# The first microseconds of an attention and feed-forward kernel: other queues, another order, other dummy matmuls

## The chip, the cores and the metric

The kernel runs on one core of a Trainium2 chip (trn2). The metric is the time of one execution in device microseconds (us); lower is better. The core's engines work side by side, each through its own list of instructions in order: TensorE (PE in the profile, with PEld for its weight loads), VectorE (DVE), ScalarE (ACT), GpSimd (POOL) and SyncE (SP). DMA transfers are issued by POOL, SP and ACT from those same lists; an issue that waits holds up everything behind it on its engine.

## The reference

Two stages follow each other. The first is a linear attention over 8 batches, 8 heads, 576 positions and 64 numbers per head; the second is a feed-forward layer with a squared ReLU.

```python
def phi(x):                                   # x: q or k
    proj = np.einsum('bhsd,df->bhsf', x, w_phi)           # 64 -> 128
    proj = proj - np.max(np.abs(proj), axis=-1, keepdims=True)
    return np.concatenate([np.exp(proj), np.exp(-proj)], axis=-1)
q_p, k_p = phi(q), phi(k)
kv = np.einsum('bhsf,bhsd->bhfd', k_p, v)
z = np.sum(k_p, axis=2)
num = np.einsum('bhsf,bhfd->bhsd', q_p, kv)
den = np.einsum('bhsf,bhf->bhs', q_p, z)[..., None] + 1e-06
x = (num / den)            # -> 4608 tokens x 512
h = np.maximum(x @ w_in, 0.0)                 # w_in: 512 x 2048
out = (h * h) @ w_out                         # w_out: 2048 x 512
```

All inputs and the output are float32; the kernel computes in bfloat16 with float32 sums.

## The kernel before, in words

**Stages.** `attention(b)` handles one batch: it transposes k and q so that the 64 numbers of a head lie on partitions, projects them with `w_phi` (the bfloat16 copy `wphi2` holds it twice, in partitions 0 to 63 and 64 to 127, so that two heads can be projected side by side), takes maxima on VectorE (`Mk`, `Mq`), exponentials on ScalarE (`Ekp`, `Ekn`), multiplies with v (`V`, `KV`), and forms the attention's output `xo`, which is transposed into `xT`. The feed-forward layer works on chunks of 512 tokens: `F1`/`f1` groups (matmuls of `win` and `xT`), ReLU and square, `F2` groups (`h` and `wout`). The attention of batch b+1 is interleaved with the feed-forward layer of the chunks before it.

**Transposes.** For batches 0 and 1, k and q are transposed on TensorE with an identity matrix `ident` (L320). From batch 2 on, SP issues transposing DMAs: kT<-xk and qT<-xq (L331). The output of batch 0 is transposed on TensorE, that of later batches by transposing DMAs xT<-xo (L708). `xo` has three buffers.

**Loads.** q, k, v, `w_in` and `w_out` are loaded by POOL, which casts them to bfloat16 on the way; at most eight of its loads are under way, each new one waits for the one eight places earlier. `xk`, `xq` and `xv` have two buffers each, so the load of batch 2 follows the last use of batch 0. Only the first heads of batch 0's k take another way: two float32 halves (128 KB each) come into the idle output buffer `ot[2]` by plain DMAs, and one `kcast` for each half turns them into bfloat16, the first on VectorE, the second on ScalarE. `w_phi` comes by a plain DMA from SP; two `wcast` write its two bfloat16 copies.

**Order.** Every operation has a number, in the order in which the program adds it. `ORDER` is a list of these numbers, written out, and `pin` chains the instructions of each engine in that order; `STATES` chooses between VectorE and ScalarE for some operations, `BASES` gives the PSUM banks, `GATES` gives some loads an operation to wait for. `FILL` puts a number of dummy matmuls (L961, on a zeroed tile `warm`) on TensorE ahead of an operation.

**The start.** In the order before: SP issues w_phi; ACT issues both k halves; POOL issues k (heads 4 to 7), q (first half), k (heads 2 and 3), then makes `ident` (L913) from a tile that VectorE zeroed (L238), then issues the second half of q, and so on. VectorE zeroes `warm`, casts the first k half, zeroes `ident`, does both `wcast`. TensorE runs 26 dummy matmuls, the four transposes of the first heads, 11 more dummies, and projects (L379).

The numbers that the diff moves: 0 and 1 are the k halves (`xkh`), 2 is w_phi, 3 and 4 the two `wcast`, 5 the zeroing of `ident`, 6 that of `warm`, 7 and 8 the two `kcast`, 11 `ident`, 12 to 14 POOL's first loads (13 is k of heads 4 to 7, 14 q, 12 k of heads 2 and 3). 303 and 304 are the two parts of the first-layer group on w_in's columns 0 to 511 for the first 128 tokens, 307/308 and 311/312 those on the next columns (512 to 1023, 1024 to 1535); 139 is a transpose of `xo`, 162, 148, 164 and 150 are L648 groups (`NA`, `NB`), 163 and 149 the scalings on VectorE (`SA`) between an `NA` and its `NB`.

Of the kernel before, what the change touches and what calls it, by code (L numbers as in the profile page):

```python
# [24 lines left out]
def dve_cost(n):  # L25
    return n / 960 + 0.064, n / 960 + 0.150 + SEM
# [82 lines left out]
def kernel(  # L109
# [10 lines left out]
    nc = tc.nc  # L120
# [97 lines left out]
    for hi in range(2):  # L218
        def fn(hi=hi):
            pin(nc.scalar.dma_start(out=ot[2][:, 256 * hi : 256 * hi + 256],  # L220
                            in_=k[0][hi, 0:512, :].rearrange("(p j) d -> p (j d)", j=4)))
        add("ACT", (0.4, 2.85), fn, w=[("xkf", hi)], what="xkh")
# [5 lines left out]
    for half in (1, 0):  # L228
        def f_wcast(half=half):
            pin(nc.vector.tensor_copy(out=wphi2[half * 64 : half * 64 + 64, :], in_=wphi_f[0:64, :]))  # L230
        add("DVE", dve_cost(64), f_wcast, r=["wphi_f"] + [("wphi2", 1)] * (1 - half), w=[("wphi2", 1) if half else "wphi2"],
            what="wcast")
# [875 lines left out]
```

## Time and profile before

| | |
|---|---|
| time, median of 3 runs | 344.13 us |
| the runs | 344.02 to 344.96 us |
| profiled execution, span from first to last instruction | 344.8 us |
| its own time beside the span | not listed apart; the span lies within the runs |
| PE busy | 335.5 us (97%) |
| DVE, ACT, POOL busy | 264.2, 225.4, 95.5 us |
| mean granted TensorE clock | 0.998 |
| HBM read, written | 36.73 MB, 9.44 MB |

In lists by time, the first number is the start in us from the start of the span, the second the time from the first start to the last end, then engine, line, operation, output<-input and the number of instructions; square brackets hold the idle time before and what ended it. "SPq" and "POOL ... DMA_DIRECT2D" are times of issuing; the transfer lands later. In lists of waits, the numbers are the total, the count and the longest wait. In lists of DMA issues the last number is the time from the start of the issue to landing, in us. Rows by stretch end with the granted clock, the share of the DMA engines and GB/s.

### The profile page before, as it was taken

What the parts mean: (1) busy time and instruction counts of PE and PEld (TensorE: products, weight loads), DVE (VectorE), ACT (ScalarE), POOL (GpSimd) and SP (SyncE); (2) the same over time, 40 slices, a digit from 0 to 9 for tenths busy, and PEclk for the clock granted to TensorE, in tenths of its full rate; (3) what the DMA queues carried; (4) which work ended last, traced back from release to release, by engine and by line L of the source; (5) the groups of instructions that cost most, each with busy time, mean ns of one, the idle gap of its engine ahead of it and who ended that gap; (6) DMA issues with size and microseconds to landing.
All of it is one profiled execution on the core that took longest, in us unless ns stands there. A gap on an engine that the chain in (4) does not pass through costs nothing.

```text
span 344.8 us, 8417 instructions
## 1 busy us (share of the span) xinstructions
PE 335.5 (97%) x3389; PEld 188.3 (55%) x3389; DVE 264.2 (77%) x485; ACT 225.4 (65%) x393; POOL 95.5 (28%) x143
## 2 busy tenths in 40 slices
PE   8999999799999999999999999999999999999995
PEld 7679776444654555545545554565555444444443
DVE  4999999699877987788898999687876635757510
ACT  4999996489898898476887797798475503210031
POOL 8670671681730390104604051240000000000000
PEclk9999999999999999999999999999999999999999
DMA  9999999999999999999999999999864821101024
GB/s 139 179 206 202 199 132 157 153 118 205 170 175 172 227 165 185 195 182 183 171 207 172 199 164 195 188 154 168 196 125 96 157 62 38 63 0 61 32 68 115
DMA packets 142935, 51.51 MB, mean 149 GB/s; under 512 B 111472, under 2 KB 138416, under 8 KB 142896
## 3 DMA queue, kind: packets, MB, share of 16 engines
q1 hardware_dynamic: 97488, 32.35, 50.7%
q0 software_dynamic: 44960, 18.23, 46.7%
q8 instruction: 26, 0.43, 0.5%
q10 hardware_dynamic: 448, 0.39, 0.4%
q14 instruction: 13, 0.11, 0.1%
HBM read 36.73 MB, written 9.44 MB: 134 GB/s over the span
## 4 chain that ended last, share of the span: by engine, by line
PE 87%; DMA 6%; DVE 3%; ACT 1%; POOL 1%; issue 0%; POOLq 0%; DVEq 0%; SPq 0%
PE psum L788 32%; PE psum L882 31%; PE psum L648 5%; PE psum L462 5%; PE psum L347 5%; DMA xT<-xo 4%; DMA qpn<-qf 3%; PE psum L827 2%; PE psum L569 1%; DVE mk L405 1%; PE psum L813 1%; PE psum L799 1%; PE psum L846 1%; PE psum L450 1%; PE psum L320 1%; PE psum L961 1%
## 5 line engine op out<-in xcount | busy, mean ns | idle before, releaser
L882 PE MATMUL psum<-wout,h 128*128 128x512 bf16 x560 | 132.6, 380 | 0.0
L788 PE MATMUL psum<-xT,win 128*128 128x512 bf16 x448 | 106.1, 379 | 0.6 <-DMA xT<-xo 0.6
L765 ACT ACTIVATE hr<-psum 128x512 bf16<-128x512 f32 x98 | 57.1, 600 | 57.7 <-PE psum L788 50.2
L882 PEld LDWEIGHTS <-h 128*128 128x128 bf16 x560 | 51.1, 98 | 56.5 <-issue 0.3
L788 PEld LDWEIGHTS <-win 128*128 128x128 bf16 x512 | 46.7, 97 | 51.9 <-DMA xT<-xo 1.4
L774 DVE TENSOR_TENSOR h<-hr 128x512 bf16<-128x512 bf16 x144 | 56.0, 415 | 18.7 <-ACT hr L765 18.2
L544 ACT ACTIVATE qf<-psum 128x1024 bf16<-128x1024 f32 (+1 forms) x50 | 46.1, 939 | 5.5 <-PE psum L347 2.0
L405 DVE TENSOR_REDUCE mk<-psum 128x8 f32<-128x1024 f32 (+1 forms) x38 | 42.4, 1120 | 3.9 <-PE psum L347 2.0
L411 ACT ACTIVATE kn<-psum 128x1024 bf16<-128x1024 f32 (+1 forms) x38 | 35.7, 948 | 8.2 <-PE psum L347 4.7
L411 ACT ACTIVATE kp<-psum 128x1024 bf16<-128x1024 f32 (+1 forms) x38 | 35.8, 951 | 4.8 <-PE psum L347 4.0
L648 PEld LDWEIGHTS <-qpn 128*128 128x128 bf16 x624 | 27.5, 97 | 16.6 <-issue 3.1
L767 DVE TENSOR_SCALAR hr<-psum 128x512 bf16<-128x512 f32 x46 | 31.1, 684 | 5.7 <-PE psum L788 4.2
L660 DVE TENSOR_TENSOR psum<-psum,en 128x520 f32<-128x520 f32 (+1 forms) x39 | 27.2, 702 | 10.3 <-PE psum L648 6.1
L648 PE MATMUL psum<-kv,qpn 128*128 128x65 bf16 x624 | 30.6, 193 | 2.5 <-DVE xo L674 2.4
L269 POOL DMA_DIRECT2D xq<-in_q_dram x24 | 17.3, 727 | 55.2 <-DVE h L774 14.3
L531 DVE TENSOR_REDUCE mq<-psum 128x8 f32<-128x1024 f32 (+1 forms) x25 | 27.8, 1112 | 3.3 <-PE psum L347 2.5
L674 DVE TENSOR_TENSOR xo<-psum,rden 128x512 bf16<-128x512 f32 (+1 forms) x39 | 26.4, 684 | 3.7 <-DMA xT<-xo 3.2
L249 POOL DMA_DIRECT2D xk<-in_k_dram x27 | 20.0, 744 | 32.5 <-ACT en L508 16.0
L584 ACT ACTIVATE qpn<-psum 128x1024 bf16<-128x1024 f32 (+1 forms) x30 | 26.8, 955 | 2.5 <-PE psum L569 2.2
L195 ACT ACTIVATE ot<-psum 128x512 f32<-128x512 f32 x24 | 14.4, 598 | 20.3 <-PE psum L882 20.1
L428 DVE TENSOR_TENSOR va<-xv,va 128x1280 bf16<-128x1280 bf16 (+2 forms) x34 | 23.4, 714 | 0.8 <-ACT va L420 0.8
L249 POOL DMA_DIRECT2D xv<-in_v_dram x27 | 19.9, 744 | 14.7 <-PE psum L788 11.1
(79 smaller groups left out, 348.9 us busy)
## 6 DMA issues: line engine op xcount, KB each, us to landing
out_dram<-ot SPq DMA_DIRECT2D x32, 256.0 KB, 2.9
xk<-in_k_dram POOLq DMA_DIRECT2D x25, 128.0 KB, 5.6
xq<-in_q_dram POOLq DMA_DIRECT2D x24, 128.0 KB, 4.5
xv<-in_v_dram POOLq DMA_DIRECT2D x24, 128.0 KB, 5.0
win<-in_moe_w_in_dram POOLq DMA_DIRECT2D x4, 512.0 KB, 9.8
wout<-in_moe_w_out_dram POOLq DMA_DIRECT2D x4, 512.0 KB, 15.1
xq<-in_q_dram POOLq DMA_DIRECT2D x4, 256.0 KB, 6.4
out_dram<-ot SPq DMA_DIRECT2D x6, 128.0 KB, 2.3
```

What stands on the lines that cost most here:

```text
L249: pin(nc.gpsimd.dma_start(out=x[:, m0 + a * 512 : m0 + z * 512].rearrange("p (h x) -> p h x", x=4 * D), in_=src[b][2 * a : 2 * z, 0:512, : ...
L405: pin(nc.vector.tensor_reduce(out=mk_view(g), in_=ps2(pj)[:, :, : n * Fd].rearrange("p e (i f) -> p e i f", f=Fd), axis=AX.X, op=ALU.max, ...
L411: pin(nc.scalar.activation(out=dst[slot][:, :, :n, :].rearrange("p e i f -> p e (i f)"), in_=ps2(pj)[:, :, : n * Fd], func=ACT.Exp, scale= ...
L531: pin(nc.vector.tensor_reduce(out=mqb[:, c, :, :n], in_=ps2(pj)[:, :, : n * Fd].rearrange("p e (i f) -> p e i f", f=Fd), axis=AX.X, op=ALU ...
L544: pin(nc.scalar.activation(out=o, in_=i_, func=ACT.Exp, scale=sgn))
L648: pin(nc.tensor.matmul(out=o[:, u // 4, u % 4 * D1 : (u % 4 + 1) * D1], lhsT=qpn[slot][:, sg * half + u * m : sg * half + u * m + P], rhs= ...
L660: pin(nc.vector.tensor_tensor(out=o, in0=o, in1=enb[:m, c, :].rearrange("t (b h) -> t b h", b=2).to_broadcast([m, 2, 4, D1]), op=ALU.mult))
L765: pin(nc.scalar.activation(out=hr[sl], in_=ps1(g), func=ACT.Relu))
L767: pin(nc.vector.tensor_scalar(out=hr[sl], in0=ps1(g), scalar1=0.0, scalar2=None, op0=ALU.max))
L774: pin(nc.vector.tensor_tensor(out=dst, in0=i_, in1=i_, op=ALU.mult))
L788: pin(nc.tensor.matmul(out=o, lhsT=win[mc // 4][:, kc, mc % 4 * P : (mc % 4 + 1) * P], rhs=x, start=(kc == 0), stop=(kc == KC - 1)))
L882: pin(nc.tensor.matmul(out=ps1(g), lhsT=h2[c % 2][mc // 4][:, mc % 4, tt * P : (tt + 1) * P], rhs=wout[mc // 4][:, mc % 4, :], start=(mc = ...
```

## The change

The second k half is issued by SP and w_phi behind it; VectorE zeroes `ident` before its cast; POOL makes `ident` behind its first load instead of its third; the first of the two `wcast` (the one for partitions 64 to 127) runs on ScalarE behind the `kcast` there; seven of the numbers of dummy matmuls differ, 17 fewer in all; and on TensorE the first-layer group 303/304 runs before 311/312 instead of after `NA` 162. Nothing else in `ORDER` differs.

```diff
     for hi in range(2):
         def fn(hi=hi):
-            pin(nc.scalar.dma_start(out=ot[2][:, 256 * hi : 256 * hi + 256],
+            pin((nc.scalar, nc.sync)[hi].dma_start(out=ot[2][:, 256 * hi : 256 * hi + 256],
                             in_=k[0][hi, 0:512, :].rearrange("(p j) d -> p (j d)", j=4)))
-        add("ACT", (0.4, 2.85), fn, w=[("xkf", hi)], what="xkh")
+        add(("ACT", "SP")[hi], (0.4, 2.85), fn, w=[("xkf", hi)], what="xkh")
...
     for half in (1, 0):
         def f_wcast(half=half):
-            pin(nc.vector.tensor_copy(out=wphi2[half * 64 : half * 64 + 64, :], in_=wphi_f[0:64, :]))
-        add("DVE", dve_cost(64), f_wcast, ...
+            copy(wphi2[half * 64 : half * 64 + 64, :], wphi_f[0:64, :])
+        add("ACT" if half else "DVE", act_cost(128) if half else dve_cost(64), f_wcast, ...
...
 ORDER = [
-    2, 0, 1, 13, 14, 12, 8, 6, 7, 5, 3, 4, 11, 19, 40, 41, ...
+    1, 0, 2, 6, 5, 13, 11, 14, 12, 8, 7, 3, 4, 19, 40, 41, ...
...
-    307, 308, 221, 147, 139, 311, 312, 309, 144, 233, 162, 313, 303, 140, 163, 304, 223, 148, 141, 164, ...
+    307, 308, 221, 147, 139, 303, 304, 311, 312, 309, 144, 233, 162, 313, 140, 163, 223, 148, 141, 164, ...
...
 FILL = {
-    40: (0, 26), 42: (0, 11), 74: (0, 5), 76: (0, 7), 58: (0, 10), 60: (4, 10), 92: (0, 7), 131: (0, 16),
+    40: (0, 22), 42: (0, 6), 74: (0, 8), 76: (0, 5), 58: (0, 11), 60: (4, 4), 92: (0, 3), 131: (0, 16),
```

In `FILL`, 40 and 42 are the first transposes and the first projection; 74 and 76 the transposes and the projection of heads 6 and 7; 58 and 60 those of heads 2 and 3; 92 transposes of q.

More of the change, by code (lines that the diff above doesn't have):

```diff
@@ L229, in f_wcast @@
         def f_wcast(half=half):
-            pin(nc.vector.tensor_copy(out=wphi2[half * 64 : half * 64 + 64, :], in_=wphi_f[0:64, :]))
-        add("DVE", dve_cost(64), f_wcast, r=["wphi_f"] + [("wphi2", 1)] * (1 - half), w=[("wphi2", 1) if half else "wphi2"],
+            copy(wphi2[half * 64 : half * 64 + 64, :], wphi_f[0:64, :])
+        add("ACT" if half else "DVE", act_cost(128) if half else dve_cost(64), f_wcast, r=["wphi_f"] + [("wphi2", 1)] * (1 - half), w=[("wphi2", 1) if half else "wphi2"],
             what="wcast")
@@ L1074 @@
 FILL = {
-    40: (0, 26), 42: (0, 11), 74: (0, 5), 76: (0, 7), 58: (0, 10), 60: (4, 10), 92: (0, 7), 131: (0, 16),
-    156: (7, 2), 101: (7, 2), 128: (7, 9), 134: (5, 4), 142: (5, 6),
+    40: (0, 22), 42: (0, 6), 74: (0, 8), 76: (0, 5), 58: (0, 11), 60: (4, 4), 92: (0, 3), 131: (0, 16), 156: (7, 2),
+    101: (7, 2), 128: (7, 9), 134: (5, 4), 142: (5, 6),
 }
```

163 rows, old and new, of the table ORDER are left out of this document.

## The prediction

> **What bounds the kernel now.** I read the page first, then the waits, then the chain of work back from the place where TensorE waits longest, then the start instruction by instruction.
>
> ```profile
> span 344.8 us, 8417 instructions
> PE 335.5 (97%) x3389; PEld 188.3 (55%) x3389; DVE 264.2 (77%) x485; ACT 225.4 (65%) x393; POOL 95.5 (28%) x143
> ```
> TensorE (PE) is busy for all but 9.3 us. The change touches only the first 32 us, so the question is which of those idle microseconds lies behind the start. The waits between 40 and 90 us give one large stall, and the chain of work shows what ended it:
>
> ```profile
> DVE xo L674 <- DMA xT<-xo: 3.2, 1, 3.2
> PE psum L648 <- DVE xo L674: 2.4, 1, 2.4
> ...
> 59.15 5.51 DMA xT<-xo
> ...
> 65.50 0.40 PE psum L648 x8
> ```
> PE stands idle from 63.1 to 65.5 us: its next matmuls (L648) need a PSUM bank that VectorE (DVE) frees at L674, and that write needs an `xo` buffer which the first transposing DMA xT<-xo reads until it lands (59.15 + 5.5 = 64.66). Why is that DMA issued only at 59.15? The timeline of SP, which issues in a fixed order, and its longest wait:
>
> ```profile
> 0.74 0.57 SPq L225 DMA_DIRECT2D wphi_f<-in_w_phi_dram  x1
> 49.81 5.17 SPq L331 DMA_TRANSPOSE kT<-xk  x1
> 55.23 3.87 SPq L331 DMA_TRANSPOSE qT<-xq  x1
> 59.15 7.51 SPq L708 DMA_TRANSPOSE xT<-xo  x4
> ...
> SPq L331 <- DMA xk<-in_k_dram: 48.3, 4, 45.9
> ```
> SP is occupied end to end from 49.81: kT, qT, then xT. And kT begins when the last piece of batch 2's k lands. That piece is the second of two behind this wait of POOL (timeline of POOL, then the landing times of the v load issued at 24.90 and of the last k pieces):
>
> ```profile
> 24.90 0.88 POOL L249 DMA_DIRECT2D xv<-in_v_dram  x1 [1.80 <-DMA win<-in_moe_w_in_dram]
> 36.54 0.70 POOL L249 DMA_DIRECT2D xk<-in_k_dram  x1 [10.75 <-PE psum L347]
> ...
> 45.88 1.41 POOL L249 DMA_DIRECT2D xk<-in_k_dram  x2 [1.22 <-DMA xq<-in_q_dram]
> ...
> xv<-in_v_dram POOLq DMA_DIRECT2D x1, 512.0 KB, 17.2
> xk<-in_k_dram POOLq DMA_DIRECT2D x2, 128.0 KB, 3.1
> ```
> The v load lands at 24.90 + 17.2 = 42.1, where a piece without a queue ahead of it needs 3.1 us: the load stream has a backlog. POOL's one wait for compute ends at 36.54, 5.5 us before the stream is through what was queued already, so issuing earlier there would bring nothing; and at 45.88 POOL waits for an earlier load, not for an engine. So 45.88, about 49.7 (the last piece) and 49.81 are set by how fast the bytes have flowed since the start. **Two strands therefore meet at 65.5 us: the engines' strand, which the change shortens, with 2.4 us in hand, and the DMA strand (loads, kT, qT, xT), which is the late one.** No other wait of PE after it is as long, so I let the end follow 65.5.
>
> **The change part by part: the start.** The timeline of the first 9 us, with the landing times of the k halves (ACT's queue), of w_phi, and of the two bf16 k loads issued at 1.25 and 2.99:
>
> ```profile
> 0.74 0.87 ACTq L220 DMA_DIRECT2D ot<-in_k_dram  x2
> 0.99 2.95 PE L961 MATMUL psum<-warm 128*128 128x128 bf16 x26 [0.99 <-DVE warm L235]
> 2.12 0.90 POOL L278 DMA_DIRECT2D xq<-in_q_dram  x1
> 2.99 0.73 POOL L249 DMA_DIRECT2D xk<-in_k_dram  x1
> 3.32 0.87 DVE L230 CAST wphi<-wphi_f 64x128 bf16<-64x128 f32 x2
> 3.60 0.42 ACT L195 ACTIVATE xk<-ot 128x256 bf16<-128x256 f32 x1 [0.67 <-DMA ot<-in_k_dram]
> 3.77 0.33 POOL L913 TENSOR_SCALAR_AFFINE_SELECT ident<-ident 128x128 bf16<-128x128 bf16 x1
> 4.16 0.59 PE L320 MATMUL psum<-ident,xk 128*128 128x128 bf16 x4 [0.21 <-POOL ident L913]
> 4.78 0.42 DVE L193 COPY kT<-psum 128x512 bf16<-128x512 bf16 x1 [0.59 <-PE psum L320]
> 5.68 0.40 PE L379 MATMUL psum<-wphi,kT 64*128 64x128 bf16 x8
> 6.15 0.69 DVE L386 TENSOR_REDUCE mk<-psum 128x4 f32<-128x512 f32 x1 [0.94 <-PE psum L379]
> 8.46 0.39 PE L320 MATMUL psum<-ident,xk 128*128 128x128 bf16 x4
> ...
> DMA to landing us min/median/max: 2.2/2.3/2.4
> wphi_f<-in_w_phi_dram SPq DMA_DIRECT2D x1, 32.0 KB, 2.5
> xk<-in_k_dram POOLq DMA_DIRECT2D x1, 128.0 KB, 5.0
> ```
> *Second half.* On ACT's queue it was issued at about 1.18 and landed at 3.58. On SP it goes out at 0.74; with the 2.2 to 2.5 us of these rows it lands at 2.94 to 3.24, I take 3.1, and ScalarE casts it until 3.1 + 0.42 = 3.5 instead of 4.0. By the Trainium skill ("DMA: Bandwidth & Descriptors", Issuing engines are not separate DMA queues) a second issuing engine saves only the issue time, here 0.44, since all transfers share 16 engines; that would put the end of the cast at 3.6, so rule and rows differ by 0.1 us here.
>
> *Identity.* Made behind POOL's first load it is ready at about 2.13 + 0.4 = 2.5 instead of 4.10, and PE's wait at 4.16 goes. Next late is ScalarE's cast: the first two transposes run after the 22 dummy matmuls, at 0.99 + 22 x 0.11 = 3.4, the last two at 3.55.
>
> *w_phi.* Issued behind the half, at about 1.3, it lands at 3.8 (was 3.24). The cast on DVE is one of the two in the row, 0.44: 3.8 to 4.25. The transposed block's copy is queued behind it and starts at about 4.25 instead of 4.78. The cast on ScalarE is not in the trace; between nothing and the 0.42 of the 128x256 cast I take 0.35, nearer to the cast, done by 4.2; projections start later than that, so it costs nothing.
>
> *Dummy runs.* Between them and the projection stand 22 and 6 matmuls instead of 26 and 11. At 2.95/26 = 0.11 us that is 1.0 us less, so the 0.43 us that PE lost between the copy's end (5.20) and 5.68 goes too. L379 then starts at about 4.7, 1.0 us earlier; the first maximum on DVE some 0.8 us earlier.
>
> *What takes part of it back.* POOL's loads issued at 2.12 and 2.99 go out 0.38 us later (the identity stands ahead of them); from 4.01 on nothing moves. The k piece issued at 2.99 landed at 8.0 and was first used at 8.46; now it lands at about 8.3, so those transposes gain only 0.1 us and DVE, which had a backlog, about 0.4. The engines' strand is then 0.4 us early, with 0.1 and 0.9 as ends.
>
> **The swap** near 29 us. Timeline:
>
> ```profile
> 28.75 0.41 PE L648 MATMUL psum<-kv,qpn 128*128 128x65 bf16 x8
> 28.99 1.06 PE L813 MATMUL psum<-xT,win 128*128 128x128 bf16 x16
> 29.32 0.70 DVE L660 TENSOR_TENSOR psum<-psum,en 128x520 f32<-128x520 f32 x1
> ```
> The second row, a first-layer group, covers the time in which DVE (third row) scales what the first L648 wrote, until 30.02, 1.27 us after that L648 began. In the new order the group runs ahead of it, and only two runs of eight L648, 0.24 each (28.75 to 28.99), are left as cover, so PE would stall for some 0.8 us. That eats the 0.4 us, and the engines' strand reaches 63 us between 0.7 late and 0.9 early (without the stall); with 2.4 us in hand either is hidden. All of the above is thus worth nothing at 65.5 us.
>
> **The load stream** is what counts. Rates in two of a row of 0.2 us stretches (last number: GB/s):
>
> ```profile
> 3.60:3.80 0.20, 0.20 (x4) 0.19 (x2) 0.19 (x2) 0.20 (x1) 0.15 (x2) 1.00 0.49 61
> 4.60:4.80 0.20, 0.20 (x5) 0.20 (x3) 0.02 (x1) 0.00 (x0) 0.20 (x1) 1.00 1.50 200
> ```
> With one load in flight 61 GB/s flow; the full 200 come with the next ones. Those go out 0.38 us later, so at worst 0.38 x (200 - 61) = 53 KB are missing, 0.26 us at 200 GB/s; at best the stream makes it up, 0. I take 0.2, near the worse end since a stream with a backlog gives nothing back. kT starts at 50.0, PE resumes at 65.7, the span grows from 344.8 to 345.0. The profile's only time for its execution is that span; it lies 0.7 above the median (344.13) and inside the runs (344.02 to 344.96), so I carry the difference over: **344.3 us**, own range 343.9 to 344.9.
>
> **The rivals.** *Head gain reaches the end.* If loads were not the bound, 0.8 us as at the first maximum would arrive: 343.3. For it speaks that up to 59 us the chain of work runs over engines and not over loads; against it the SP rows above. It needs kT to start at 49.0.
>
> *Slower: loads in front of xT.* POOL's next loads are released by compute at 59 us and share the engines with the first xT:
>
> ```profile
> 59.06 0.63 POOL L257 DMA_DIRECT2D xk<-in_k_dram  x1 [8.33 <-ACT en L508]
> ...
> 61.17 0.71 POOL L269 DMA_DIRECT2D xq<-in_q_dram  x1
> ```
> These are four loads, two of 32 and two of 128 KB: 1.6 us at 200 GB/s. If the engines' strand is early by about 0.8 us, more of them run ahead of xT, which is late by up to 1.6; I price it at 1.2: 345.3. Against it: POOL's pace, not that one release, sets most of them. The mirror image, a late strand and loads that fall behind xT, gives 342.9; for it speaks only the 0.8 us of the swap.
>
> *Clock.*
>
> ```profile
> 7.89 0.73 PE L961 MATMUL psum<-warm 128*128 128x128 bf16 x10
> ```
> Dummy matmuls need 0.11 us each at the start, and here, with 0.2 us for the last one's way through the array, (0.73 - 0.2)/9 = 0.06; the change of pace lies near 5.3 us, while the granted clock reads 1.00 throughout; so a cold spell like that from 1.0 to 5.3 costs half of 4.3, 2.1 us. The stall of 2.4 us did not bring it back; an early strand and a late stream make it longer, and from some length above 2.4 that no row shows the end would be 346.4. The Trainium skill ("TensorE: Matmul & The Clock Gate", Part 1: The HAM clock gate) has the clock halve after an idle window of about 3.4 us, which takes a strand 0.8 early and a stream 0.2 late; the trace agrees so far, as 2.4 left the pace alone.
>
> That the change doesn't do what it says (the half no sooner on SP) ends at 344.3 too, and is in the first case.
>
> **How the numbers follow.** Chances: forecast 0.50, head gain 0.17, loads ahead 0.17, loads behind 0.10, clock 0.06. 0.3% is 1.03 us, about what a measurement of this kernel tells from no change. Faster by more: half of the head gain (its bound is 1.0, the start of L379), all of "behind", 0.01 of the first: 0.20. Slower by more: clock, 0.15 of "ahead", 0.03 of the first: 0.24. Within: 0.56. The range 343.0 to 345.6 leaves out the clock, most of "behind" and the edges of the others, 0.2 in all.
>
> **What would show it.** Right: first transposes near 3.5, L379 near 4.7, the wait at 29.9 new, kT on SP within 49.8 to 50.1, and PE's wait at L648 ending near 65.7 whatever its length. Wrong: kT earlier than 49.5 (the stream was not the bound), xT landing more than 0.5 us off 14.9 after kT's start (contention), or matmuls at half pace after 65 us.

## The result, and the profile after

| | kernel before | changed kernel |
|---|---|---|
| median of 12 runs each, on one chip | 344.58 us | 347.65 us |
| lowest to highest | 343.79 to 348.06 us | 346.53 to 350.76 us |
| ratio, 95% interval | | 1.0085 (1.0060 to 1.0109) |

The change costs 0.85%. The forecast was 344.3 us, within 343.0 and 345.6.

One thing about the profiles first. The list of runs gives span and time side by side: the changed kernel's profiled execution has a span of 346.8 us and a time of 348.58, and every other run shows the same 1.8 us between the two. The profile of before, with its span of 344.8, is thus an execution of about 346.6 us, two above its median. Where a profile and a median point different ways below, the median decides.

The page of the changed kernel begins:

```profile
span 346.8 us, 8353 instructions
PE 334.5 (96%) x3342; PEld 188.8 (54%) x3372; DVE 264.0 (76%) x484; ACT 225.8 (65%) x394; POOL 95.5 (28%) x143
```

TensorE is busy for 1.0 us less (17 dummies are gone) in a span 2.0 us longer, so in these two profiles it stands idle for 3.0 us more. The start in order of time, with rows left out:

```profile
0.74 0.39 SPq L220 DMA_DIRECT2D ot<-in_k_dram  x1
0.99 2.53 PE L961 MATMUL psum<-warm 128*128 128x128 bf16 x22 [0.99 <-DVE warm L235]
1.19 0.56 SPq L225 DMA_DIRECT2D wphi_f<-in_w_phi_dram  x1
2.21 0.31 POOL L913 TENSOR_SCALAR_AFFINE_SELECT ident<-ident 128x128 bf16<-128x128 bf16 x1
2.45 0.91 POOL L278 DMA_DIRECT2D xq<-in_q_dram  x1
3.36 0.42 ACT L195 ACTIVATE xk<-ot 128x256 bf16<-128x256 f32 x1 [0.89 <-DMA ot<-in_k_dram]
3.53 0.29 DVE L193 CAST xk<-ot 128x256 bf16<-128x256 f32 x1 [2.51 <-DMA ot<-in_k_dram]
3.88 0.61 PE L320 MATMUL psum<-ident,xk 128*128 128x128 bf16 x4 [0.36 <-DVE xk L193]
4.28 0.85 PE L961 MATMUL psum<-warm 128*128 128x128 bf16 x6
4.58 0.31 ACT L195 ACTIVATE wphi<-wphi_f 64x128 bf16<-64x128 f32 x1 [0.80 <-DMA wphi_f<-in_w_phi_dram]
4.72 0.41 DVE L193 COPY kT<-psum 128x512 bf16<-128x512 bf16 x1
5.19 0.61 PE L379 MATMUL psum<-wphi,kT 64*128 64x128 bf16 x8
5.73 1.04 PE L961 MATMUL psum<-warm 128*128 128x128 bf16 x8
5.86 0.69 DVE L386 TENSOR_REDUCE mk<-psum 128x4 f32<-128x512 f32 x1 [0.73 <-PE psum L379]
...
ot<-in_k_dram SPq DMA_DIRECT2D x1, 128.0 KB, 2.6
ot<-in_k_dram ACTq DMA_DIRECT2D x1, 128.0 KB, 2.8
...
wphi_f<-in_w_phi_dram SPq DMA_DIRECT2D x1, 32.0 KB, 3.4
```

The last three rows are the landing times. The identity is ready at 2.5 and the first transposes begin 0.3 us earlier (3.88 for 4.16), the projection 0.5 earlier (5.19 for 5.68), the first maximum 0.3 earlier (5.86 for 6.15). TensorE now waits 0.36 us ahead of the transposes, for VectorE's cast of the half that ACT issued (3.53 + 0.29 = 3.82); the half on SP is cast by 3.78. Then the weight loads of TensorE between 5.9 and 8.7 us, by line and form (the last number before the bar is the mean of one in ns), before and after:

```profile
L961 PEld LDWEIGHTS <-warm 128*128 128x128 bf16 x22 | 1.3, 98 | 0.2
L320 PEld LDWEIGHTS <-xk 128*128 128x128 bf16 x12 | 0.8, 98 | 0.0
```
```profile
L961 PEld LDWEIGHTS <-warm 128*128 128x128 bf16 x11 | 1.3, 152 | 0.0
L320 PEld LDWEIGHTS <-xk 128*128 128x128 bf16 x8 | 0.9, 152 | 0.0
```

The same load of the same tile takes 152 ns instead of 98: in this execution TensorE is still at its slow pace, which in the profile of before ended at 5.4 us. It ends at 9.2 us here. By 12 us the engines are 1.0 us behind those of before. The swap, near 30 us:

```profile
28.96 1.95 PE L813 MATMUL psum<-xT,win 128*128 128x128 bf16 x32
30.75 0.41 PE L648 MATMUL psum<-kv,qpn 128*128 128x65 bf16 x8
30.95 0.60 ACT L765 ACTIVATE hr<-psum 128x512 bf16<-128x512 f32 x1 [0.97 <-PE psum L813]
31.60 0.82 PE L648 MATMUL psum<-kv,qpn 128*128 128x65 bf16 x16 [0.44 <-ACT hr L765]
```

The new stall is there. It ends with a relu on ScalarE (30.95 + 0.60) that frees a PSUM bank. Then the loads on POOL, the transposing DMAs on SP, and the waits between 40 and 90 us:

```profile
38.41 0.70 POOL L249 DMA_DIRECT2D xk<-in_k_dram  x1 [12.05 <-PE psum L347]
...
47.45 1.43 POOL L249 DMA_DIRECT2D xk<-in_k_dram  x2 [2.43 <-DMA xq<-in_q_dram]
...
51.33 4.66 SPq L331 DMA_TRANSPOSE kT<-xk  x1
56.22 4.60 SPq L331 DMA_TRANSPOSE qT<-xq  x1
60.87 4.26 SPq L708 DMA_TRANSPOSE xT<-xo  x3
...
DVE xo L674 <- DMA xT<-xo: 2.3, 1, 2.3
PE psum L648 <- DVE xo L674: 1.5, 1, 1.5
```

POOL's wait for a projection ends 1.9 us later than before (36.54), the load for kT goes out 1.6 later (45.88), kT starts 1.5 later (49.81), and TensorE resumes at 66.52 instead of 65.50, although it stands still for less. Both strands have moved.

### The profile page after: what moved, and what is told of

Same layout as the page of the kernel before. It is cut to its first block, busy times and chain, and to the rows that moved or that the text cites. A ratio compares the mean times of both kernels' runs of the same rounds, so it can differ in the third digit from the quotient of the medians.

```text
span 346.8 us, 8353 instructions
## 1 busy us (share of the span) xinstructions
PE 334.5 (96%) x3342; PEld 188.8 (54%) x3372; DVE 264.0 (76%) x484; ACT 225.8 (65%) x394; POOL 95.5 (28%) x143
## 4 chain that ended last, share of the span: by engine, by line
PE 88%; DVE 4%; DMA 4%; ACT 2%; issue 1%; SPq 0%; DVEq 0%
PE psum L882 33%; PE psum L788 29%; PE psum L648 5%; PE psum L347 5%; PE psum L462 5%; PE psum L827 2%; DMA xT<-xo 1%; PE psum L569 1%; DMA out_dram<-ot 1%; PE psum L813 1%; PE psum L799 1%; PE psum L846 1%; DMA wphi_f<-in_w_phi_dram 1%; PE psum L961 1%; PE psum L450 1%
## 5 line engine op out<-in xcount | busy, mean ns | idle before, releaser
L882 PE MATMUL psum<-wout,h 128*128 128x512 bf16 x530 | 128.5, 379 | 2.0 <-issue 0.6
L674 DVE TENSOR_TENSOR xo<-psum,rden 128x512 bf16<-128x512 f32 (+1 forms) x39 | 26.4, 684 | 2.8 <-DMA xT<-xo 2.3
```

What stands on the lines that cost most here:

```text
L882: pin(nc.tensor.matmul(out=ps1(g), lhsT=h2[c % 2][mc // 4][:, mc % 4, tt * P : (tt + 1) * P], rhs=wout[mc // 4][:, mc % 4, :], start=(mc = ...
```

## The experiments

Each ratio is to the kernel before, run on the same chip.

### Which part costs the time

**e1_no_swap**, the changed kernel with the first-layer order of before:

```diff
-    ... 147, 139, 303, 304, 311, 312, ... 162, 313, 140, 163, 223, ...
+    ... 147, 139, 311, 312, ... 162, 313, 303, 140, 163, 304, 223, ...
```

> The changed kernel with the first-layer group 303/304 back at its old place; all else changed. If the swap is the cause (it exposes the scaling on VectorE and a PSUM bank near 30 us, about 0.8 us of PE, which the load gate near 36 us hands on), this is 0.8 to 2 us faster than the changed kernel, about 346, and the wait of L648 near 30 us is gone. If the cause is the start (cold clock, w_phi late), it stays within 0.5 us of the changed kernel, about 347.3.

Measured: 347.31 us, 1.0066 (1.0042 to 1.0089). Most of the loss stays.

**e2_swap_only**, the kernel before with that one exchange (the diff above, the other way round).

> The kernel before with the swap alone. Swap as cause: slower than before by 0.8 to 2 us, about 345.5 to 346.5, POOL's load at line 249 that waits for PE issued 0.7 to 1 us later, kT later by as much. Start as cause, or the stall near 63 us as a cushion: within 0.3 us of before.

Measured: 345.30 us, 1.0003 (0.9979 to 1.0027). The swap alone can't be told from no change.

**e3_old_dummies**, the changed kernel with the dummy numbers of before:

```diff
-    40: (0, 22), 42: (0, 6), 74: (0, 8), 76: (0, 5), 58: (0, 11), 60: (4, 4), 92: (0, 3),
+    40: (0, 26), 42: (0, 11), 74: (0, 5), 76: (0, 7), 58: (0, 10), 60: (4, 10), 92: (0, 7),
```

> The changed kernel with the numbers of dummy matmuls of before (17 more). Clock as cause: dummy matmuls go to half their time near 5.3 us again instead of near 8.9, and the time falls by about 1 us or more, to 346.5 or less, although PE has more to do. Swap or w_phi as cause: no change, 347 to 348, or slower by the dummies' 0.5 to 1 us.

Measured: 345.48 us, 1.0021 (1.0008 to 1.0034). Three quarters of the loss are gone.

**e4_new_dummies_only**, the kernel before with the new numbers (the same diff reversed).

> The kernel before with the changed numbers of dummy matmuls alone. Clock as cause: a gap of 0.5 us or more ahead of the first transposes, a clock that stays at half pace for some 3.4 us longer in most runs, and 1 us or more slower than before. Otherwise: within 0.3 us of before, or faster by some 0.4 us since the dummies between the copy and L379 are gone.

Measured: 347.26 us, 1.0063 (1.0033 to 1.0093): 17 dummy matmuls fewer, and nothing else, cost 0.6%. Its weight loads between 5.9 and 8.7 us:

```profile
L961 PEld LDWEIGHTS <-warm 128*128 128x128 bf16 x13 | 1.4, 146 | 0.2 <-issue 0.2
L320 PEld LDWEIGHTS <-xk 128*128 128x128 bf16 x8 | 0.9, 152 | 0.0
```

They are slow too, without any change of queues or order.

**e8_queues_only**, the changed kernel with the dummies and the first-layer order of before (both diffs); what is left are the queues, the identity and the cast.

> The queues, the identity and the casts as changed, with the dummies and the order of the first-layer groups of before. The changed kernel with old dummies and this one differ by the swap alone. Prediction's view: 0.2 us slower than before (load stream) or the same. If the later landing of the first bf16 k load (6.1 to 6.4 us instead of 5.7) and of the stream behind it (0.5 us) reaches the end: 0.5 us slower. If the swap is harmless, the same as the changed kernel with old dummies, 345.5.

Measured: 344.91 us, 1.0012 (0.9997 to 1.0028): it can't be told from the kernel before. In its profile the write to `xo` at L674 near 60 us, which serves as a mark of the engines' strand from here on, starts at 60.33, 0.14 later than in that of before; the earlier start is worth nothing there.

### Which of the dummies

**e5_first_dummies_back** (changed kernel):

```diff
-    40: (0, 22), 42: (0, 6),
+    40: (0, 26), 42: (0, 11),
```

> The changed kernel with the first two numbers of dummy matmuls as before (26 and 11 instead of 22 and 6), the others changed. If gaps of TensorE ahead of the first transposes and the first projection keep the clock at half pace: no gap at 3.5 us, full pace near 5.5 us, and about 345.5, 2 us under the changed kernel. If the later dummies (8 us on) matter, it stays near 347.

Measured: 345.69 us, 1.0032 (1.0013 to 1.0052).

**e6_late_dummies_back** (changed kernel):

```diff
-    74: (0, 8), 76: (0, 5), 58: (0, 11), 60: (4, 4), 92: (0, 3),
+    74: (0, 5), 76: (0, 7), 58: (0, 10), 60: (4, 10), 92: (0, 7),
```

> The changed kernel with the other five numbers as before, the first two (22 and 6) changed. First gaps as cause: the gap at 3.5 us stays, half pace until about 9 us in most runs, 347 to 348. Later dummies as cause: about 345.5.

Measured: 346.33 us, 1.0049 (1.0022 to 1.0075).

**e10_close_first_gap** (changed kernel, `40: (0, 26)` alone).

> The changed kernel with 26 instead of 22 dummies ahead of the first transposes; the transposes wait for the k halves until 3.9 us anyway, so nothing on the path moves, the gap of 0.36 us is closed. If the share of the clock's window in which TensorE works decides: full pace by 7 us in every run, about 345.7, 2 us under the changed kernel. If the second number (6 instead of 11) or the later ones matter by themselves: 346.5 to 347.5.

Measured: 346.86 us, 1.0048 (1.0021 to 1.0076).

**e7_first_gap** (kernel before, `40: (0, 22)` alone).

> The kernel before with 22 instead of 26 dummies ahead of the first transposes and nothing else: TensorE then idles for 0.64 us instead of 0.21 there. If one such gap is enough for the clock: half pace until about 8.9 us in many runs and a median 1 us or more above before. If not: within 0.3 us of before, and the second number (6 instead of 11) is needed too.

Measured: 344.75 us, 1.0011 (0.9991 to 1.0031). The first number by itself costs nothing that can be told (e7). Of the tests that put numbers back, the two ahead of the first projection together recover most; the intervals of the three overlap, so a finer split stays open, and the other numbers were not tried one by one.

### The clock at the start

**e9_cold_start**, the kernel before with 18 of the first 26 dummies gone, so that TensorE stands idle for 2 us at the start:

```diff
-    40: (0, 26),
+    40: (0, 8),
```

> The kernel before with 8 instead of 26 dummies ahead of the first transposes, nothing else: no window of 3.4 us before 7 us can be busy enough, so the clock goes to full pace at 7 to 10 us in every run, while loads, queues and all later dummies stay. Late clock as the cause of the slowdown: 1 us late after the start in the trace, median 1.5 to 2.5 us above before, 346 to 347. If a late start is absorbed near 63 us and the slowdown comes otherwise (fewer late dummies, order of events): within 0.5 us of before.

Measured: 348.32 us, 1.0108 (1.0061 to 1.0156). These dummies end long before the first transposes, which start at 4.16 in this profile as they do in that of before, so no work of the kernel is nearer or farther for them. What they change is what TensorE has done before; without them the full pace comes at 7.7 us in the profile (5.4 in that of before), and the kernel is about as slow as the changed one.

The trace's records of the clock say when the full pace comes. In e1 the clock fell once more, after a stall of 2.41 us at 108.4, and the time by stretches (the number behind POOL is the granted clock) shows it:

```profile
108.40:112.00 3.60, 1.22 (x6) 0.60 (x7) 1.15 (x1) 0.59 (x3) 0.00 (x0) 1.00 1.15 166
112.00:115.40 3.40, 3.40 (x10) 1.21 (x8) 2.96 (x6) 2.67 (x6) 0.00 (x0) 0.50 0.98 214
115.40:119.00 3.60, 3.60 (x59) 2.19 (x58) 2.00 (x5) 1.70 (x4) 1.18 (x2) 1.00 1.11 235
```

The low clock lasts 3.41 us (111.98 to 115.39), and from the first rise at 6.16 to the fall at 111.98 are 31 times 3.41. In the other 17 profiles the high clock lasts 334.5, 337.9 or 341.3 us, 98, 99 or 100 times 3.413, and then falls near the kernel's end or behind it. So it is decided window by window. I took, for every profile, the windows of 3.41 us that end at the first rise and the ones before it, and the share of each in which TensorE streamed (each matmul counted to the next one's start, at most 107 ns, which is the usual distance of two starts at the slow pace; at the full one it is 56). Over the 18 profiles:

| window | full pace after it |
|---|---|
| share 0.778 to 0.965 (17 windows) | in all 17 |
| 0.746 (e1) | yes |
| 0.760 (e15), 0.750 (e14), 0.716 (changed kernel), 0.702 (e4), 0.671 (e7) | no |

The windows before these, most of them ahead of the first matmul, have shares of 0.63 or less, and none brought it.

So a window needs TensorE busy for about three quarters; the one at 0.746 shows that this share, or the border, is not exact. The grid of these windows does not start with the kernel: the first rise lies anywhere from 4.4 to 10.0 us. With 26 dummies at the start the full pace came between 4.4 and 7.0 us in all nine profiles; with 22 it came at 9.0 to 10.0 in three of eight (changed kernel, e4, e7) and between 4.9 and 7.6 in the others. The Trainium skill ("TensorE: Matmul & The Clock Gate", Part 1: The HAM clock gate) has this free-running window of about 3.4 us, and the traces agree with it (3.41). The same section of the Trainium skill puts the start-up penalty below 1% of a typical span. Between the earliest and the latest first rise (4.4 and 10.0 us) the lost pace is about half of 5.6 us, by estimate 2.8 us or 0.8% of this kernel, so the traces agree; the whole matter here is about 1%.

**e11_look_b** and **e12_look_c** are the changed kernel again, unchanged, for more than one draw of that grid.

> The changed kernel once more, one look at the trace: where the clock goes to full pace this time. By the windows, either at 4 to 7.5 us (then the engines are level with before by 10 us) or at 9 to 10.5 us (then 1 us late), depending on where the window lies.

> As the look before: a third trace of the changed kernel, for the place of the clock's change and for the stalls near 65 and 110 us. If the slowdown is the late clock alone, a trace with an early change is not slower than 346 us.

Measured: 347.78 and 347.41 us, with full pace at 5.4 and 4.9 us. So the late clock is **not** the whole loss: two executions in which it came early are as slow as the others. Nor does it cost that much wherever it comes: in e7's profile the full pace came latest of all, at 10.0 us, and that execution took 345.80 us. In e11 TensorE waited 1.01 us at 8.5 us for a k load, and was almost as late afterwards (61.79 at the mark for 62.06). In e12 the engines were late only by the swap at 60 us, as in e3, and lost 1.6 us at one place later:

```profile
111.38 4.06 PE L788 MATMUL psum<-xT,win 128*128 128x512 bf16 x18 [1.60 <-DMA xT<-xo]
```

where e3 lost 0.5. What lies behind that place comes at the end of the next section.

### Whether a late start grows

What remained was how 1 to 2 us at the start become 3 at the end. The next two kernels delay the engines where the clock is up and nothing else is touched: more dummies near 25 us, in the kernel before.

**e13_late_1us** and **e14_late_2us**:

```diff
-    156: (7, 2), 101: (7, 2), 128: (7, 9), 134: (5, 4), 142: (5, 6),
+    156: (7, 2), 101: (7, 2), 128: (7, 9), 134: (5, 4), 142: (5, 23),   # e14: 40
```

> The kernel before with 17 more dummy matmuls ahead of operation 142 (number 6 becomes 23). That lies near 25 us, after the clock has come up, and TensorE has no idle time between there and 60 us, so the engines' strand is 17 x 0.06 = 1.0 us later from 25 us on with nothing else changed. Theory P (a late strand is passed on nearly whole: some 0.5 us is in hand near 63 us in a usual execution, the 2.4 us of the first profile was not usual): ratio 1.001 to 1.003, near 345.3. Theory G (a late strand is made larger by the load that waits for it on POOL at 36.5 us): a wait that ends at 37.6 doesn't move the transposing DMA kT, which starts near 49.8, so no more than P here. Rival (2.4 us in hand absorb it): 1.000.

> The kernel before with 34 more dummy matmuls ahead of operation 142 (6 becomes 40): the strand is 34 x 0.06 = 2.1 us later from 25 us on, about as late as in the changed kernel's profile, without a change at the start and without the swap. Theory P: near 346.3, ratio 1.004 to 1.005. Theory G: POOL's wait ends near 38.6, kT starts near 51.3, and the end is more than the 2.1 us late: 347.3 or more, ratio 1.007 or more, like the changed kernel. Rival (absorbed): 1.000 to 1.001.

Measured: e13 345.76 us, 1.0021 (1.0000 to 1.0042); e14 348.56 us, 1.0097 (1.0059 to 1.0135). Twice the delay costs more than twice as much by the ratios (0.7 us, then 3.3), though by the ends of the intervals it could be anything above 1.4 times. The rows of POOL's wait and of kT on SP, e13 (its execution took 349.07 us, the longest of its runs) and then e14:

```profile
37.41 0.70 POOL L249 DMA_DIRECT2D xk<-in_k_dram  x1 [11.84 <-PE psum L347]
...
50.30 4.64 SPq L331 DMA_TRANSPOSE kT<-xk  x1
```
```profile
38.88 0.70 POOL L249 DMA_DIRECT2D xk<-in_k_dram  x1 [13.34 <-PE psum L347]
...
52.71 4.34 SPq L331 DMA_TRANSPOSE kT<-xk  x1
```

**e15_gate**, the changed kernel with that load released by an earlier projection:

```diff
-    355: 3, 356: 170, 357: 152,
+    355: 3, 356: 196, 357: 152,
```

> The changed kernel with the load of batch 2's k that waits on POOL for operation 170 (a projection of q near 37.8 us) waiting for operation 196 instead (the projection of k near 34.8 us, 3 us earlier). The engines' strand is as late as before. Theory G: with POOL's wait ended at about 35.5, kT starts at 49.8 again, and 0.8 to 1.5 us of the loss are gone: near 346.4, ratio 1.004 to 1.006. Theory P (the strand's lateness alone is passed on): kT earlier or not, the time stays at 347.6, ratio 1.008.

Measured: 345.99 us, 1.0047 (1.0011 to 1.0083); five of its ten runs lie between 344.7 and 345.6, below every run of the changed kernel (346.53). Its profile:

```profile
34.74 0.70 POOL L249 DMA_DIRECT2D xk<-in_k_dram  x1 [7.97 <-PE psum L347]
...
50.46 4.34 SPq L331 DMA_TRANSPOSE kT<-xk  x1
```

With the load released 3.7 us sooner kT starts 0.9 sooner than in the profile of the changed kernel, and the median is 1.7 us lower. By the medians this is about half of the loss, from one number that alters only when loads are issued. But the intervals of the two ratios overlap, so the gain is likely and not shown; and the profiled execution, with its earlier kT, took 349.03 us, no less than that of the changed kernel (348.58).

**e16_queues_gate**, the same number in e8, where the engines are not late.

> The queues, identity and cast of the changed kernel with the dummy numbers and the first-layer order of the kernel before (344.9 by an earlier run), with the same earlier wait for batch 2's k load as in the kernel above. The prediction held that an earlier issue there brings nothing, since the stream has a backlog until 42 us: then kT stays at 49.7 to 49.9 and the time at 1.000 to 1.002. If the wait did hold the stream up, kT starts up to 1 us sooner and the ratio is 0.997 to 0.999.

Measured: 344.96 us, 1.0022 (0.9992 to 1.0051). kT starts at 49.33, 0.5 us sooner than in e8's profile, but the time is no better: where the strand is on time the earlier release brings nothing at the end.

Put side by side, all profiles whose load is released as in the kernel before (the first four columns are of the one profiled execution, the last is from all runs):

| kernel | L674 near 60 us | POOL's wait ends | kT starts | time of this execution | ratio |
|---|---|---|---|---|---|
| before | 60.19 | 36.54 | 49.81 | about 346.6 | 1 |
| e1 | 60.19 | 36.54 | 49.68 | 347.79 | 1.0066 |
| e8 | 60.33 | 36.67 | 49.81 | 345.48 | 1.0012 |
| e6 | 60.94 | 37.29 | 50.23 | 344.62 | 1.0049 |
| e3 | 61.01 | 37.36 | 49.73 | 344.91 | 1.0021 |
| e10 | 61.05 | 37.40 | 50.32 | 345.31 | 1.0048 |
| e9 | 61.06 | 37.41 | 50.49 | 348.46 | 1.0108 |
| e13 | 61.06 | 37.41 | 50.30 | 349.07 | 1.0021 |
| e12 (changed) | 61.11 | 37.46 | 49.43 | 347.41 | 1.0085 |
| e2 | 61.14 | 37.49 | 49.26 | 347.07 | 1.0003 |
| e5 | 61.17 | 37.52 | 50.26 | 344.77 | 1.0032 |
| e4 | 61.37 | 37.71 | 50.16 | 346.67 | 1.0063 |
| e11 (changed) | 61.79 | 38.14 | 51.06 | 347.78 | 1.0085 |
| e7 | 61.85 | 38.20 | 50.09 | 345.80 | 1.0011 |
| changed kernel | 62.06 | 38.41 | 51.33 | 348.58 | 1.0085 |
| e14 | 62.53 | 38.88 | 52.71 | 348.21 | 1.0097 |

Up to 37.7 us the wait goes with a kT between 0.6 us early and 0.7 us late. Of the four waits that end beyond 38 us, three go with a kT 1.2 to 2.9 us late, and one, e7's, with 0.3. So a late wait can make kT late, but does not have to. And the time does not follow this path alone: e1 and e12 are slow with kT on time, e9 is slow with kT 0.7 us late, and e7, as late at the mark as e11, loses nothing that can be told.

What the six profiles with all seven new numbers (changed kernel, e1, e4, e11, e12, e15) have in common lies later. In each of them TensorE stops once for 1.0 to 2.4 us between 108 and 117 us; in the other twelve no stop there is longer than 0.8. Ahead of it SP issues kT, one other transposing DMA and then the xT that e1, e4, e12 and e15 wait for. From the start of that kT to that of xT SP takes 7.9 to 8.7 us in the six, and 5.2 to 7.4 in the twelve; before and then e12:

```profile
98.69 3.86 SPq L331 DMA_TRANSPOSE kT<-xk  x1
102.67 1.33 SPq L548 DMA_TRANSPOSE qpn<-qf  x1
104.10 3.31 SPq L708 DMA_TRANSPOSE xT<-xo  x2
```
```profile
97.90 4.91 SPq L331 DMA_TRANSPOSE kT<-xk  x1
102.92 2.95 SPq L548 DMA_TRANSPOSE qpn<-qf  x1
105.97 2.53 SPq L708 DMA_TRANSPOSE xT<-xo  x2
```

In e1 the stop, with the low clock that followed it, is all of the loss: at L674 its engines are 0.9 us ahead of those of e8 at 105.79 us and 2.7 behind at 121.26. So the engines need not be late for it. This is a pattern found in one execution of each kernel, and the profiles of e5, e6 and e10 were among the quickest of their runs; how dummy matmuls of the first 12 us reach SP's issues near 100 us is not known.

No version beat the kernel before: e2, e7, e8 and e16 can't be told from it.

## Why the prediction was wrong, step by step

**Dummy runs: the step that failed.** They were counted as "1.0 us less" work ahead of the projection. They also keep TensorE busy enough for the full pace; without them it came late in three of eight profiles with 22 at the start and in none of nine with 26, depending on how the grid falls. e4 (only the dummies, 1.0063) and e3 (all but the dummies, 1.0021) show that taking them away is the main cost: a saving, hidden later behind the DMA strand, was entered where e4 shows a loss of about 2 us. e9 (1.0108) shows that dummies far ahead of any wait count too. The prediction had both paces in its rows (0.11 and 0.06 us a matmul) and took the change of pace, 5.3 us, as given, although the change removes matmuls from the very microseconds ahead of it. It put the clock's danger at the stall near 63 us, at 6%; it belonged to the start. That the late clock is at most part of the dummies' cost is shown by e11 and e12, slow with an early clock; how the rest of the cost comes about stays open.

**"2.4 us in hand": mis-sized.** That stall was of one execution, two microseconds slower than the median. In the profile of e8, where L674 near 60 us starts within 0.14 us of that of before, TensorE stood still for 0.9 us there, so in that execution there was that much in hand. It differs from one execution to the next: in e7's profile the engines are 1.7 us later than in that of before, the profile lists no wait of TensorE there, and the execution took 345.80. The failed sub-step is the last one: the span was compared with the median of times, "0.7 above", when 1.8 us lie between a span and its time.

**POOL's wait at 36.54 "brings nothing": right for an earlier one, not for a later one.** In e16 an earlier one brought kT 0.5 us and the end nothing. The prediction concluded from a backlog of 5.5 us that this wait does not matter. It has 1 to 2 us in hand, not 5.5 (e11, e14 and the changed kernel against the rest of the table): the pieces for kT are issued one behind the other only after it, and POOL's next wait for a load moved from 45.88 to 47.45. This is a path by which a late engines' strand can make the DMA strand late as well; the prediction kept the two apart until 65.5 us. What it costs the changed kernel is not clear of the noise (e15). Its rivals had a late strand only as a gain, 342.9.

**Second half, w_phi, casts.** Forecast 3.1 and measured 3.34 for the half on SP; ACT's half, issued at 0.74 as before, took 2.8 us to land where the row of before has 2.3. The transposes waited for that one, not for the half on SP. w_phi landed at 4.56, forecast 3.8: 3.4 us in place of 2.5, behind a half on its own queue (2.5 to 3.4 in the eleven profiles with these queues). The cast on ScalarE took 0.31 us, forecast 0.35. The projection came 0.5 us earlier, forecast 1.0, and the first maximum 0.3, forecast 0.8. The Trainium skill's rule that the prediction weighed ("DMA: Bandwidth & Descriptors", Issuing engines are not separate DMA queues) had the cast end at 3.6; it ended at 3.36 + 0.42 = 3.78 on ScalarE, so rows (3.5) and rule were both too early, the rule by less.

**Load stream, 0 to 0.26 us.** The loads at 2.12 and 2.99 went out at 2.45 and 3.35, as forecast. But the first k load in bfloat16, issued at 1.25 in both kernels, needed 5.1 us where it had needed 4.4:

```profile
xk<-in_k_dram POOLq DMA_DIRECT2D x1, 256.0 KB, 5.1
```

In the eleven profiles with the new queues it took 4.8 to 5.2, in six of the seven with the old ones 4.4 to 4.7 and in e9 5.1. That the two halves, now issued at the same moment, hold it up is likely; the prediction did not count it. e8 shows that this costs nothing measurable at the end.

**Swap, 0.8 us.** The marks show 0.6 to 0.7 (e3 against e8 at 60 us: 0.68), near enough; the wait behind it was a relu that frees a bank, not the scaling. That "either is hidden" was tested by e2 (1.0003) and held within the interval there. Whether it counts on top of fewer dummies is not shown: e1 without it is at 1.0066 for 1.0085, and the intervals overlap.

**Clock, rival.** "From some length above 2.4" was right in kind: e1's stall of 2.41 us halved the clock for one window, 3.41 us, which is 1.7 us of lost pace. The idle window of 3.4 us that the prediction worked with was not needed. The stall of 2.37 in the profile of before halved nothing. The two are nearly of one length; on the grid, 2.2 us of e1's fall into one window (108.56 to 111.98, TensorE busy for 35% of it) and 2.0 us of the other (63.46 to 66.87, 40%). That the place on the grid decides and not the length fits the start, but these two can't separate them.

**What stays open.** How fewer dummies at the start cost 2 us at the end. The late clock, kT behind POOL's wait and the stop near 110 us are each seen in some slow executions; only the last is in all six profiles with the seven new numbers. e9 and e14 bring about the first and the second by themselves, on a larger scale, and are slow; how much of the changed kernel's loss either carries is not shown, and nothing was tried on the third.

## What to carry to other kernels

Dummy matmuls at the start are not filler to be trimmed to the wait they cover: measure their removal by itself, as e4 does, and work out for every position of the 3.4 us window whether TensorE is still busy for three quarters of it. Before relying on slack that one profile shows, compare its span, with the fixed part added, with the median of the runs, and look at the same place in a second profile. And where a load is released by compute, ask for the latest time at which that release does no harm, not only whether an earlier one would help. Before an account is built on a few profiles, put all of them into its table: the one that doesn't fit says how far it goes.

## What the runs showed of the hardware that was not expected

The granted clock of a profile does not show the slow pace at the start: the changed kernel's mean is 1.000, and its stretch from 5.8 to 9.2 us reads 1.00, while its weight loads take 152 ns for 98.

```profile
5.80:9.20 3.40, 3.40 (x39) 3.01 (x40) 2.60 (x5) 2.10 (x5) 3.30 (x6) 1.00 1.71 176
```

Transfers issued on different queues at about the same time are not independent: ACT's half, issued at 0.74 in both kernels and first on its queue, took 2.7 to 2.8 us to land in the eleven profiles in which SP issues the other half at the same moment. In the seven in which ACT issues both, the median of the two is 2.2 to 2.5.
